# S4D block in front of a feed-forward net: the written order on GpSimd, the initial sums after the odd sines, and a setup in three parts

## The chip, the cores and the metric

The kernel runs on one core of one Trainium2 chip. The metric is the device time of one execution in microseconds; less is better. The three runs shown below took 1494.46, 1496.56 and 1498.57 us; their median, 1496.56 us, is the time before. The profile was taken of a further execution, which took 1500.85 us.

A core has a matrix engine (TensorE, PE in the profile; its weight loads are PEld), VectorE (DVE), ScalarE (ACT), GpSimd (POOL) and SyncE (SP), which only issues transfers here. Each engine works through its own queue in order; an instruction whose input is not there yet holds up all that is queued behind it.

## The reference

```python
mod = (silu(c) @ w_mod)                      # 6 vectors of 576: sa, ca, ga, sb, cb, gb
dt = exp(log_dt);  A = -exp(log_A_real) + 1j*A_imag;  C = (C_real + 1j*C_imag)*dt
P = exp((A*dt)[:, :, None] * pos)            # 576 channels x 128 states x 2048 positions
K = 2*einsum("dn,dnl->dl", C, P).real        # one filter of 2048 taps for each channel
h = layernorm(x)*(1+ca) + sa
x = x + ga*(causal_convolution(h, K) + h*D_skip)
h = layernorm(x)*(1+cb) + sb
x = x + gb*(relu(h @ w1) @ w2)               # 2048 x 576, inner width 4608
```

All is in float32.

## The kernel before

The positions are cut into four blocks of 512. Kernel block 0 (the first 512 taps of all filters, class KGen) is computed first, in about 197 us; then the convolution of block 0, and then the feed-forward net, during which the filters and convolutions of the later blocks run beside the matrix products. This text is about the first 197 us.

**Groups.** The 576 channels are six groups of 96; g is the group. A complex power exp((A dt) l) is taken apart by position: l is written as the sum of a part that W1 holds (positions in steps of 32, 16 of them) and a part that W2 holds (32 offsets around it). The products of the two, summed over the 128 states, are matrix products.

**One group goes through these steps.**
- `turns(g)`: matrix products of angles (`zt`) with a diagonal of positions (`dl`) give the angle in turns in a PSUM bank (tile `ph`); ScalarE rounds it to an integer (`k`), VectorE subtracts (line 143). Six chunks, two in each of three tiles.
- `exps(g)`: ten chunks of matrix products with `zr`; ScalarE takes the exponential (`E`).
- `values(g)`: sines and cosines on ScalarE; the sine products with E on VectorE (lines 179 and 180), the cosine products on GpSimd (lines 184 and 185), once for odd and once for even positions. For the odd ones `start` also makes the first entry of W1, out of the coefficients `cc`: `tc` on GpSimd (line 201), `Tc` on VectorE (line 202), and the two initial sums on VectorE (lines 203 and 204). `powers` makes the multipliers `Zp` and `zs`.
- `doubling(g)`: W1 grows from one entry to 16 in four steps, each two products and two sums. The sums of the last step, in two halves u0 and u1, are done by GpSimd (lines 246 and 247), all others by VectorE.
- `products(g)`: 384 small matrix products (line 255), the first 192 from u0 and the others from u1, into one PSUM bank (`kps`). `rows` copies it out (`ke`).

**The written order** in `first` is: the loads of `mod` and silu(c), spread over a tile `cb`; turns and exps of group 0; the product for ga (`mps_ga`); values(0); turns and exps of group 1; the product for ca (`mps_ca`). Then for each g: doubling(g), products(g) (for g = 0 the product for sa, `mps_sa`, follows), values(g+1), turns and exps of g+2.

**What sets the real order.** A scheduler goes through the program with a model of the machine; of what the model holds to be ready, an engine gets the instruction that is written first. So an engine's queue can differ from the written order. `keep_in_program_order` ties an instruction behind the one that was written before it on its engine. Before the change, only ScalarE's activations in this stage are tied (helper `act`, line 49; all of them have that line in the profile).

**Shared buffers.** Three PSUM banks `ph` serve turns, exps, the mod products and `kps`. The sine tile `s` has one buffer, so the even sines wait until the odd sine products have read it. The tag W1 has two buffers: the weights `wm_ga` and `wm_ca` lie in them before W1 of groups 0 and 1.

Of the kernel before, what the change touches and what calls it, by code (L numbers as in the profile page):

```python
# [18 lines left out]
P = 128  # L19
# [20 lines left out]
class KGen:  # L40
# [7 lines left out]
    def act(self, *args, **kw):  # L48
        return self.tc.keep_in_program_order(self.nc.scalar.activation(*args, **kw))
# [10 lines left out]
    def setup(self, I):  # L60
        nc, pc, k = self.nc, self.pc, self.k
        v = nc.vector.tensor_tensor
        tmp = lambda n: self.pt.tile([G, NG, P], F32, tag="W2", bufs=5, name=n)
# [17 lines left out]
        th = self.pt.tile([G, NG, P], F32, tag="T1", bufs=2, name="th")  # L81
        z = [pc.tile([G, 2, NG, P], F32R, name=f"z{n}") for n in "tr"]
        v(ai, ai, dtb, op=ALU.mult)
        nc.vector.tensor_scalar(th, ai, TURN_LO, None, op0=ALU.mult)
        nc.vector.scalar_tensor_tensor(th, ai, TURN_HI, th, op0=ALU.mult, op1=ALU.add)
        self.act(z[0][:, 0], th, AF.Copy)
        self.diag(lv, slice(0, 8))
        v(z[0][:, 1], th, z[0][:, 0], op=ALU.subtract)
# [7 lines left out]
        self.zz = z  # L96
        self.act(dt, dt, AF.Exp)
        for r in range(2):
            nc.vector.scalar_tensor_tensor(
                self.cc[:, r], self.cc[:, r], 2.0 - 4.0 * r, dt, op0=ALU.mult, op1=ALU.mult  # L100
            )

    def diag(self, lv, sl):
        n = sl.stop - sl.start
        self.nc.vector.tensor_tensor(
            self.dl[:, sl],
            self.k.ident[:G, :G].unsqueeze(1).broadcast_to([G, n, G]),
            lv[:, sl].unsqueeze(2).broadcast_to([G, n, G]),
            op=ALU.mult,
        )  # L110
# [46 lines left out]
    def half_values(self, g, W2, E, f, odd):  # L157


        nc = self.nc  # L160
        v, p = nc.vector.tensor_tensor, nc.gpsimd.tensor_tensor
        j0 = 0 if odd else 16
# [11 lines left out]
        if odd:  # L174
            self.start(g, su[:, :, 7], c[:, 7])
        for u in range(2):
            uc = slice(u * H, u * H + H)
            hi, lo = slice(j0 + 8, j0 + 16), slice(j0, j0 + n)
            v(W2[u][:, 1, hi], su[:, u], Eh[:, :, uc], op=ALU.mult)
            nc.vector.scalar_tensor_tensor(  # L180
                W2[u][:, 1, lo][:, ::-1], su[:, u, 0:n], -1.0,
                El[:, 0:n, uc][:, ::-1], op0=ALU.mult, op1=ALU.mult,
            )
            p(W2[u][:, 0, hi], c[:, :, uc], Eh[:, :, uc], op=ALU.mult)
            p(W2[u][:, 0, lo][:, ::-1], c[:, 0:n, uc], El[:, 0:n, uc][:, ::-1], op=ALU.mult)
            if not odd:
                nc.gpsimd.tensor_copy(W2[u][:, 0, 23], El[:, 7, uc])
                nc.gpsimd.memset(W2[u][:, 1, 23], 0.0)

    def start(self, g, s15, c15):  # L190

        v, p = self.nc.vector.tensor_tensor, self.nc.gpsimd.tensor_tensor
        W1 = self.W1[g] = self.pt.tile([P, 2, 16, 2, H], F32, tag="W1", bufs=2, name=f"W1_{g}")
# [8 lines left out]
        v(T, cc, s15.unsqueeze(1).broadcast_to(cb), op=ALU.mult)  # L202
        v(W1[:, :, 0, 0], t[:, 0], T[:, 1], op=ALU.add)
        v(W1[:, :, 0, 1], t[:, 1], T[:, 0], op=ALU.subtract)

    def powers(self, g, e, f):

        v, p = self.nc.vector.tensor_tensor, self.nc.gpsimd.tensor_tensor
        Z = self.ps.tile([P, 2, 512], F32, tag="Z", name=f"Zp_{g}")[:, :, 0 : 4 * G]
# [12 lines left out]
    def doubling(self, g):  # L222

        v, p = self.nc.vector.tensor_tensor, self.nc.gpsimd.tensor_tensor
        W1, Z = self.W1[g], self.Z[g][0]
# [36 lines left out]

    def first(self, mod):

# [160 lines left out]
class Body:  # L425
# [3 lines left out]
    def build(self):  # L429
        nc, tc, I = self.nc, self.tc, self.I  # L430
        with ExitStack() as ctx:
# [14 lines left out]
            with ExitStack() as c2:  # L446
                kg.open(c2)
                kg.setup(I)
                kg.first(self.mod(kg))
            self.main(ctx, kg)  # L450
# [16 lines left out]
    def mod(self, kg):  # L467
# [17 lines left out]
        self.mod_lhs(cb)  # L485
        yield
        self.m = {}
# [592 lines left out]
```

## Time and profile before

| | us |
|---|---|
| median of three runs | 1496.56 |
| the profiled execution, device time | 1500.85 |
| its span, first to last instruction | 1499.0 |
| kernel block 0, to the last copy of `ke` | 0 to 193.4 |
| products of groups 0 to 5 begin at | 49.9, 82.0, 108.0, 134.4, 161.7, 179.5 |
| TensorE busy / VectorE / ScalarE / GpSimd, whole span | 88% / 62% / 32% / 11% |

In rows of the timeline the first two numbers are the start and the length in us, then come engine, line, operation, output<-inputs, shape and count; in brackets stands how long the engine had been idle and what ended that. A row with a count merges neighbours; its length goes from the start of the first to the end of the last. "issue" is a wait that no semaphore explains. In rows of the windows view each engine has its busy time and its instructions; after them come the granted TensorE clock, the share of time that the transfer engines were busy, and GB/s.

### The profile page before, as it was taken

How to read it: one execution, taken by the hardware profiler on the slowest of the kernel's cores; microseconds unless marked ns; L12 is line 12 of the kernel's file. 1: busy time of each engine (PE TensorE's matmuls, PEld its weight loads, DVE VectorE, ACT ScalarE, POOL GpSimd, SP SyncE). 2: the span in 40 equal slices, each digit the busy share in tenths (PEclk: the TensorE clock that was granted, in tenths of full speed). 3: DMA queues.
4: the chain of work that ended last, by engine and by line, in shares of the span. 5: the costliest groups of instructions: out<-in, count | busy, mean ns of one | idle time of the engine just before them, and what ended most of it. 6: DMA issues, size and time to landing. Idle time of an engine off the chain costs nothing.

```text
span 1499.0 us, 26182 instructions
## 1 busy us (share of the span) xinstructions
PE 1314.2 (88%) x10664; PEld 1037.4 (69%) x10664; DVE 928.2 (62%) x1392; ACT 481.4 (32%) x889; POOL 168.7 (11%) x271
## 2 busy tenths in 40 slices
PE   5976547599998996788999998999999999999997
PEld 3665434477776764566777776787787888888885
DVE  6576649899946398684884597727599822111112
ACT  5475432222221242133223422334322333233331
POOL 2346500000021100001101000000000000000000
PEclk9755569699999998789999999999999999999998
DMA  4535666367598664647976889566799566766662
GB/s 157 212 154 218 229 230 244 136 230 268 182 351 315 212 244 186 258 150 265 354 239 228 314 304 357 165 215 206 283 324 385 173 184 203 210 194 194 198 191 72
DMA packets 118120, 345.99 MB, mean 231 GB/s; under 512 B 19633, under 2 KB 23377, under 8 KB 106993
## 3 DMA queue, kind: packets, MB, share of 16 engines
q1 hardware_dynamic: 99648, 218.88, 44.8%
q0 software_dynamic: 18128, 124.86, 22.1%
q8 instruction: 83, 1.36, 0.4%
q10 hardware_dynamic: 224, 0.59, 0.1%
q14 instruction: 37, 0.30, 0.1%
HBM read 260.53 MB, written 83.76 MB: 230 GB/s over the span
## 4 chain that ended last, share of the span: by engine, by line
PE 43%; DVE 23%; issue 19%; DMA 9%; ACT 3%; POOL 1%; SPq 0%; POOLq 0%; ACTq 0%; DVEq 0%
PE acc L902 15%; PE hps L877 14%; PE kps L381 4%; DVE T L742 4%; DVE Y L744 4%; PE ps_f L613 3%; PE ph L117 3%; DMA Ud<-U 2%; PE kps L255 2%; DMA L1d<-w 1%; PE ps_i L751 1%; DMA kt<-kd 1%; DMA Ua<-Ud 1%; DVE T L350 1%; DVE Y L738 1%
## 5 line engine op out<-in xcount | busy, mean ns | idle before, releaser
L902 PE MATMUL acc<-hh,w 128*128 128x512 f32 x1296 | 428.6, 405 | 4.7 <-DMA w<-L2d 3.7
L877 PE MATMUL hps<-xh,w 128*128 128x512 f32 x1152 | 394.5, 403 | 0.0
L902 PE MATMUL acc<-hl,w 128*128 128x512 f32 x720 | 283.5, 407 | 20.3 <-DVE hl L883 20.3
L883 DVE SCALAR_TENSOR_TENSOR hl<-hps,hh 128x512 fp32r<-128x512 f32 x144 | 98.8, 686 | 310.5 <-ACT hh L882 310.2
L902 PEld LDWEIGHTS acc<-hh,w 128*128 128x128 f32 x1296 | 245.9, 191 | 59.7 <-DMA w<-L2d 4.5
L877 PEld LDWEIGHTS hps<-xh,w 128*128 128x128 f32 x1152 | 219.0, 191 | 47.5
L877 PE MATMUL hps<-xl,w 128*128 128x512 f32 x576 | 232.3, 403 | 0.0
L882 ACT ACTIVATE hh<-hps 128x512 fp32r<-128x512 f32 x144 | 86.1, 598 | 353.2 <-PE hps L877 349.8
L860 ACT ACTIVATE w<-r 128x576 fp32r<-128x576 f32 x144 | 98.8, 686 | 278.0 <-issue 183.9
L902 PEld LDWEIGHTS acc<-hl,w 128*128 128x128 f32 x720 | 137.2, 191 | 50.7 <-DVE hl L883 21.5
L877 PEld LDWEIGHTS hps<-xl,w 128*128 128x128 f32 x576 | 110.3, 192 | 23.8
L851 ACT ACTIVATE w<-r 128x640 fp32r<-128x640 f32 x144 | 105.4, 732 | 24.4 <-DMA L1d<-w 20.5
L877 PE MATMUL hps<-xs,w 128*128 128x512 f32 x288 | 101.0, 420 | 10.8 <-DMA w<-L1d 5.2
L381 PEld LDWEIGHTS kps<-W1r,W2r 128*32 128x32 f32 x3456 | 68.8, 146 | 39.3 <-issue 28.3
L381 PE MATMUL kps<-W1r,W2r 128*32 128x48 f32 (+2 forms) x3456 | 79.5, 238 | 14.3 <-issue 12.3
L744 DVE TENSOR_TENSOR Y<-Y,T 128x1152 f32<-128x1152 f32 x64 | 84.5, 1347 | 0.1
L255 PE MATMUL kps<-W,W 128*32 128x16 f32 x2304 | 42.0, 218 | 42.6 <-issue 21.2
L614 ACT ACTIVATE Z<-ps_f 128x288 f32<-128x288 f32 x128 | 51.7, 409 | 70.7 <-PE ps_f L613 67.9
L255 PEld LDWEIGHTS kps<-W,W 128*32 128x32 f32 x2304 | 39.2, 151 | 47.3 <-issue 22.2
L877 PEld LDWEIGHTS hps<-xs,w 128*128 128x128 f32 x288 | 54.0, 192 | 25.7 <-DMA w<-L1d 6.8
L1000 POOL DMA_DIRECT2D out_dram<-x x16 | 8.7, 546 | 511.9 <-DVE x L998 511.9
L613 PE MATMUL ps_f<-kt,fcK 128*128 128x288 f32 x128 | 45.0, 450 | 21.2 <-DMA wm_sb<-in_w_mod_dram 15.5
(177 smaller groups left out, 1545.4 us busy)
## 6 DMA issues: line engine op xcount, KB each, us to landing
r<-in_w_dram SPq DMA_DIRECT2D x144, 320.0 KB, 3.7
r<-in_w_dram SPq DMA_DIRECT2D x144, 288.0 KB, 3.5
w<-L1d SPq DMA_DIRECT2D x108, 320.0 KB, 3.1
w<-L2d SPq DMA_DIRECT2D x108, 288.0 KB, 3.2
W2r<-W2d POOLq DMA_DIRECT2D x18, 1536.0 KB, 9.0
W2d<-W SPq DMA_DIRECT2D x12, 1536.0 KB, 7.2
Ua<-Ud POOLq DMA_DIRECT2D x15, 1152.0 KB, 10.5
W<-W1d POOLq DMA_DIRECT2D x18, 768.0 KB, 10.2
```

The costliest lines, as they stand in the source:

```text
L255: self.nc.tensor.matmul(ps[32 * dd : 32 * dd + 32, 12 * u + q, :], W2[:, r, :, ch], W1[:, u, :, r, ch], start=(r == 0), stop=(r == 1),)
L381: nc.tensor.matmul(ps[32 * dd : 32 * dd + 32, q, :], W2[:, r, :, ch], W1[:, :, r, ch], start=(r == 0), stop=(r == 1),)
L613: nc.tensor.matmul(o, fc[:, n2, c, :], src(n2), start=True, stop=True)
L614: nc.scalar.activation(Z[:, n2, c], ps[:, :PC], AF.Copy)
L742: v(T, k, u, op=ALU.mult)
L744: v(y, y, T, op=op or ALU.add)
L851: nc.scalar.activation(w[:, 0], r, AF.Copy)
L860: nc.scalar.activation(w[:, 0:D], r, AF.Copy)
L877: nc.tensor.matmul(ps, a, x, start=(i == 0), stop=(i == 13))
L882: nc.scalar.activation(hh, ps, AF.Relu)
L883: nc.vector.scalar_tensor_tensor(hl, ps, 0.0, hh, op0=ALU.max, op1=ALU.subtract)
L902: nc.tensor.matmul(acc[i], a, x, start=(f == 0 and j in (0, 3, 6, 9, 12)), stop=(f == NF - 1 and j in (2, 5, 8, 11, 13)),)
```

## The change

- GpSimd's two-input operations in this stage (`start`, `half_values`, `powers`, `doubling`) are tied to the written order. So the u1 sums of doubling(g) come ahead of `tc` and of the cosine products of group g+1, and these ahead of the sums of doubling(g+1).
- In the odd half of `values`, the initial sums (lines 203 and 204) are written behind the four odd sine products, and the cosine products after them. The sums themselves stay free.
- The setup is cut in three. What turns(0) needs stays in front and is tied in order. Part 2 (the decay rates `lar`, `zr`, two pieces of the diagonal) comes between turns(0) and exps(0). Part 3 (exp of dt, the coefficients `cc`) comes after exps(0).
- In `mod`, the exponential of c, the rest of silu and `cb` move behind the first `yield`: after part 3, ahead of the product for ga.

```diff
+    def pool(self, out, a, b, op):
+        self.tc.keep_in_program_order(self.nc.gpsimd.tensor_tensor(out, a, b, op=op))
...
-        v(ai, ai, dtb, op=ALU.mult)
-        nc.vector.tensor_scalar(th, ai, TURN_LO, None, op0=ALU.mult)
-        nc.vector.scalar_tensor_tensor(th, ai, TURN_HI, th, op0=ALU.mult, op1=ALU.add)
+        kept(v(ai, ai, dtb, op=ALU.mult))
+        kept(nc.vector.tensor_scalar(th, ai, TURN_LO, None, op0=ALU.mult))
+        kept(nc.vector.scalar_tensor_tensor(th, ai, TURN_HI, th, op0=ALU.mult, op1=ALU.add))
         self.act(z[0][:, 0], th, AF.Copy)
         self.diag(lv, slice(0, 8))
-        v(z[0][:, 1], th, z[0][:, 0], op=ALU.subtract)
+        kept(v(z[0][:, 1], th, z[0][:, 0], op=ALU.subtract))
         self.diag(lv, slice(16, 25))
-        nc.vector.scalar_tensor_tensor(lar, lar, -1.0, dtb, op0=ALU.mult, op1=ALU.mult)
-        self.act(z[1][:, 0], lar, AF.Copy)
         self.diag(lv, slice(32, NS))
-        v(z[1][:, 1], lar, z[1][:, 0], op=ALU.subtract)
-        self.diag(lv, slice(8, 16))
-        self.diag(lv, slice(25, 32))
...
+        def part2():
+            kept(nc.vector.scalar_tensor_tensor(lar, lar, -1.0, dtb, op0=ALU.mult, op1=ALU.mult))
+            self.act(z[1][:, 0], lar, AF.Copy)
+            v(z[1][:, 1], lar, z[1][:, 0], op=ALU.subtract)
+            self.diag(lv, slice(8, 16))
+            self.diag(lv, slice(25, 32))
+
+        def part3():
+            self.act(dt, dt, AF.Exp)
+            for r in range(2):
+                nc.vector.scalar_tensor_tensor(
+                    self.cc[:, r], self.cc[:, r], 2.0 - 4.0 * r, dt, op0=ALU.mult, op1=ALU.mult
+                )
+
+        return part2, part3
...
-        v, p = nc.vector.tensor_tensor, nc.gpsimd.tensor_tensor
+        v, p = nc.vector.tensor_tensor, self.pool
...
         if odd:
-            self.start(g, su[:, :, 7], c[:, 7])
+            ends = self.start(g, su[:, :, 7], c[:, 7])
         for u in range(2):
             ...
             v(W2[u][:, 1, hi], su[:, u], Eh[:, :, uc], op=ALU.mult)
             nc.vector.scalar_tensor_tensor(...)
+        if odd:
+            for out, a, b, op in ends:
+                v(out, a, b, op=op)
+        for u in range(2):
+            uc = slice(u * H, u * H + H)
             p(W2[u][:, 0, hi], c[:, :, uc], Eh[:, :, uc], op=ALU.mult)
...
         def raw(g, then=lambda: None):
             F = self.turns(g, then)
+            if g == 0:
+                setup[0]()
             EF[g] = self.exps(g), F
+            if g == 0:
+                setup[1]()
...
             self.mod_weights(w, slice(i * D, (i + 1) * D))
+        yield
         kg.act(ex, ct, AF.Exp, scale=-1.0)
...
         self.mod_lhs(cb)
-        yield
```

`diag` ties its product in the same way, and `start` hands its two sums back instead of issuing them.

More of the change, by code (lines that the diff above doesn't have):

```diff
@@ L81, in setup @@
         th = self.pt.tile([G, NG, P], F32, tag="T1", bufs=2, name="th")
-        z = [pc.tile([G, 2, NG, P], F32R, name=f"z{n}") for n in "tr"]
-        v(ai, ai, dtb, op=ALU.mult)
-        nc.vector.tensor_scalar(th, ai, TURN_LO, None, op0=ALU.mult)
-        nc.vector.scalar_tensor_tensor(th, ai, TURN_HI, th, op0=ALU.mult, op1=ALU.add)
+        z = self.zz = [pc.tile([G, 2, NG, P], F32R, name=f"z{n}") for n in "tr"]
+        kept(v(ai, ai, dtb, op=ALU.mult))
+        kept(nc.vector.tensor_scalar(th, ai, TURN_LO, None, op0=ALU.mult))
@@ L94, in setup @@
-        self.diag(lv, slice(8, 16))
-        self.diag(lv, slice(25, 32))
[L96 to L101, printed above, removed]
+        def part2():
[4 more added lines that the diff above has]
+            self.diag(lv, slice(25, 32))
@@ L103, in diag @@
+        def part3():
[5 more added lines that the diff above has]
+        return part2, part3
     def diag(self, lv, sl):
         n = sl.stop - sl.start
[L105 to L109, printed above, removed]
+        self.tc.keep_in_program_order(
+            self.nc.vector.tensor_tensor(
+                self.dl[:, sl],
+                self.k.ident[:G, :G].unsqueeze(1).broadcast_to([G, n, G]),
+                lv[:, sl].unsqueeze(2).broadcast_to([G, n, G]),
+                op=ALU.mult,
+            )
@@ L202, in start @@
         v(T, cc, s15.unsqueeze(1).broadcast_to(cb), op=ALU.mult)
-        v(W1[:, :, 0, 0], t[:, 0], T[:, 1], op=ALU.add)
-        v(W1[:, :, 0, 1], t[:, 1], T[:, 0], op=ALU.subtract)
+        return (
+            (W1[:, :, 0, 0], t[:, 0], T[:, 1], ALU.add),
+            (W1[:, :, 0, 1], t[:, 1], T[:, 0], ALU.subtract),
+        )
     def powers(self, g, e, f):
-        v, p = self.nc.vector.tensor_tensor, self.nc.gpsimd.tensor_tensor
+        v, p = self.nc.vector.tensor_tensor, self.pool
         Z = self.ps.tile([P, 2, 512], F32, tag="Z", name=f"Zp_{g}")[:, :, 0 : 4 * G]
@@ L222, in doubling @@
     def doubling(self, g):
-        v, p = self.nc.vector.tensor_tensor, self.nc.gpsimd.tensor_tensor
+        v, p = self.nc.vector.tensor_tensor, self.pool
         W1, Z = self.W1[g], self.Z[g][0]
@@ L261, in products, with first @@
                     )
-    def first(self, mod):
+    def first(self, setup, mod):
         nc, k = self.nc, self.k
@@ L447, in build @@
                 kg.open(c2)
-                kg.setup(I)
-                kg.first(self.mod(kg))
+                setup = kg.setup(I)
+                kg.first(setup, self.mod(kg))
             self.main(ctx, kg)
```

6 lines of the change are left out of this document (3 added, 3 removed).

## Prediction

> **What bounds the kernel now.** I read the page first, then the windows view by stages, then the chain of waits and the timeline of the first 200 us. After 260 us nothing of the change runs, and TensorE is busy for 1147 of 1239 us; what the first stage gains or loses is carried to the end one for one. So only the first 193 us count.
>
> ```profile
> span 1499.0 us, 26182 instructions
> ...
> 260.00:1499.00 1239.00, 1147.12 (x7968) 906.09 (x7968) 755.23 (x1034) 355.30 (x656) 76.97 (x137) 0.96 0.70 236
> ```
>
> The first stage is a relay. TensorE's products(g) are followed by turns(g+2) in TensorE's own queue; VectorE's queue has the subtractions of these turns ahead of most of doubling(g+1); this leads to GpSimd's sums and to products(g+1). The next rows show the products of groups 1, 2 and 3.
>
> ```profile
> 88.45 2.36 PE L255 MATMUL kps<-W,W 128*32 128x16 f32 x128 [2.31 <-issue]
> ...
> 93.10 1.40 PE L255 MATMUL kps<-W,W 128*32 128x16 f32 x68 [2.29 <-issue]
> ...
> 113.54 0.94 PE L255 MATMUL kps<-W,W 128*32 128x16 f32 x39 [2.05 <-issue]
> 115.15 1.60 PE L255 MATMUL kps<-W,W 128*32 128x16 f32 x89 [0.67 <-POOL W L247]
> 117.85 1.87 PE L255 MATMUL kps<-W,W 128*32 128x16 f32 x101 [1.10 <-issue]
> ...
> 135.37 3.10 PE L255 MATMUL kps<-W,W 128*32 128x16 f32 x190
> 139.84 0.30 PE L255 MATMUL kps<-W,W 128*32 128x16 f32 x2 [1.38 <-POOL W L246]
> 140.80 2.95 PE L255 MATMUL kps<-W,W 128*32 128x16 f32 x183 [0.66 <-POOL W L247]
> 146.61 0.42 PE L255 MATMUL kps<-W,W 128*32 128x16 f32 x7 [2.86 <-issue]
> ```
>
> TensorE stalls after each run of 128 products (x128, and 39 + 89) without a semaphore, and runs begin 4.65 (88.45 to 93.10) or 4.31 us (113.54 to 117.85) apart. 128 products with their loads are 256 instructions; the queue of instruction loading moved 20 packets in this stage:
>
> ```profile
> q8 instruction: 20, 0.33, 0.7%
> ```
>
> So I read these stalls as the loading of the next 256 instructions, and a run of products as bound by it at some 4.3 to 4.7 us per 128. A sum that comes earlier inside a run buys nothing.
>
> **GpSimd's order.** No work is added. In group 3 the u0 sums end at 135.32 and the u1 sums' inputs are there by then, but `tc` and two cosine products come first:
>
> ```profile
> 134.32 1.00 POOL L247 TENSOR_TENSOR W<-T,T 128x384 f32<-128x384 f32 x1
> 136.25 0.62 POOL L201 TENSOR_TENSOR tc<-cc,c 128x192 f32<-128x192 f32 x1 [0.93 <-ACT c L49]
> ```
>
> Tied, the u1 sums follow at 135.3 and end at 137.2, while now they release TensorE at 140.80; `tc` starts at 137.2, 1.0 later; what is queued behind the cosine products ends 1.0 earlier, since the idle 0.93 is used. Who waits for `tc` is VectorE's line 203, which moves back too. SP's queue gets the store of W1 some 3.5 us earlier and the one of W2 no later; nothing in this stage reads them. For TensorE: group 1 had no wait for GpSimd, gain 0. In group 2 the wait (0.67) lies within the run that began at 113.54, and the next comes 4.31 later anyway: 0. In group 3 the waits are 1.38 + 0.66. The run that ends in the 2.86 stall began 128 products before 143.75, at about 141.7; without the waits it could begin when its instructions are there, one spacing (4.3) after the run before it (119 products in, 137.3), at 141.6. That makes a gain of 0.1 at least and 2.0 at most; I take 1.0, since 141.7 showed no stall and the loading may have been done well before. Group 4's products are followed by no turns, so its gain lies on no path. **−1.0** (−2.0 to 0).
>
> **Initial sums behind the odd sines.** For the last groups VectorE waits for `tc` in the middle of the odd sine products, and ScalarE's even sines wait for the last of these:
>
> ```profile
> 162.45 0.55 DVE L179 TENSOR_TENSOR W<-s,E 128x384 f32<-128x384 f32 x1
> 164.20 0.26 DVE L203 TENSOR_TENSOR W<-tc,Tc 128x96 f32<-128x96 f32 x1 [1.21 <-POOL tc L201]
> ...
> 164.54 0.55 DVE L180 SCALAR_TENSOR_TENSOR W<-s,E 128x384 f32<-128x384 f32 x1
> ...
> 166.05 0.81 ACT L49 ACTIVATE s<-k 128x768 f32<-128x768 f32 x1 [1.90 <-DVE W L180]
> ```
>
> Behind the sines, line 180 follows line 179 at 162.92 (0.47 from start to start) instead of 164.54: 1.6 earlier. In groups 1 to 3 what ends earlier (multipliers, ScalarE's queue) then waits for TensorE's turns: nothing gained. After group 4 there are no more turns: even sines, multipliers, doubling(5) and products(5) hang on it in line: **−1.6** (0 if the sums stay early, at most the 1.90).
>
> **Setup.** These rows carry it:
>
> ```profile
> 5.14 0.56 DVE L84 TENSOR_SCALAR th<-ai 96x768 f32<-96x768 f32 x1
> 6.19 0.84 ACT L49 ACTIVATE lar<-lar 96x768 f32<-96x768 f32 x1 [2.63 <-DMA lar<-in_lar_dram]
> 7.94 0.95 DVE L85 SCALAR_TENSOR_TENSOR th<-ai,th 96x768 f32<-96x768 f32 x1
> 9.81 0.95 DVE L88 TENSOR_TENSOR zt<-th,zt 96x768 fp32r<-96x768 f32 x1
> 10.41 0.67 ACT L49 ACTIVATE dt<-dt 128x576 f32<-128x576 f32 x1
> 10.68 1.72 DVE L105 TENSOR_TENSOR dl<-ident,lv 96x864 fp32r<-96x864 f32 x2
> 11.54 0.87 ACT L49 ACTIVATE k<-ph 128x384 int32<-128x384 f32 x2 [0.37 <-PE ph L117]
> 14.83 1.42 DVE L99 SCALAR_TENSOR_TENSOR cc<-cc,dt 128x576 f32<-128x576 f32 x2
> 16.24 0.55 DVE L143 TENSOR_TENSOR k<-ph,k 128x384 f32<-128x384 f32 x1
> 17.77 0.81 DVE L513 COPY cb<-ct 128x640 f32<-128x640 f32 x1
> 18.50 1.27 DVE L143 TENSOR_TENSOR k<-ph,k 128x384 f32<-128x384 f32 x3
> 19.10 5.95 PE L117 MATMUL ph<-dl,zr 96*128 96x384 f32 x20 [0.29 <-DVE k L143]
> 20.14 5.40 ACT L49 ACTIVATE E<-ph 128x384 f32<-128x384 f32 x10 [0.89 <-PE ph L117]
> 24.99 5.70 PE L518 MATMUL mps_ga<-wm_ga,cb 128*128 128x288 f32 x20
> 26.85 0.81 ACT L49 ACTIVATE s<-k 128x768 f32<-128x768 f32 x1
> ```
>
> Line 85 follows line 84 at 5.7 and ends at 6.6. ScalarE's copy to zt waits for `lar` (7.03) and, like it, takes 0.84: 7.9. Line 88 ends at 8.85, the two pieces of the diagonal (1.72) at 10.5. The first k came 0.78 after line 88's end, so at 9.6. The first subtraction thus starts at 10.5, not 16.24; all six took 3.5 (to 19.77), so they end at 14.0. Then part 2, alone on the path: multiply 0.95, copy 0.84, subtract 0.95, with TensorE idle: exps(0) at 16.8, not 19.10, **2.3 earlier**. E ends at 23.2. Behind it ScalarE now has dt (0.67) and the small exponential of c (five columns, an estimated 0.1), which ran under VectorE's setup before; the sines, 1.31 after E now, start at 25.3, **1.5 earlier** than 26.85.
>
> The cover that is gone is that of `cb`. dt is done at 23.8, `cc` takes 1.42, three small steps an estimated 0.4, `cb` 0.81: 26.4, so `mps_ga` starts 1.4 later than now, and TensorE idles from 22.7 to 26.4. What an idle stretch like that does to its clock shows here:
>
> ```profile
> 35.62 1.97 PE L117 MATMUL ph<-dl,zt 96*128 96x384 f32 x6 [3.67 <-DVE k L143]
> ...
> 59.47 10.04 PE L518 MATMUL mps_sa<-wm_sa,cb 128*128 128x288 f32 x20
> ```
>
> ```profile
> 34.30:44.20 9.90, 8.37 (x26) 7.71 (x27) 9.57 (x24) 7.60 (x16) 4.68 (x7) 0.50 0.77 318
> ...
> 59.50:68.50 9.00, 9.00 (x20) 5.52 (x18) 2.38 (x6) 0.00 (x0) 0.89 (x2) 0.50 0.81 308
> ```
>
> After 3.67 idle the granted clock was 0.50 until 44.2, and `mps_sa`, the same 20 products as `mps_ga`, took 10.04 at 0.50 against 5.70. I take 10.04, the nearest row: `mps_ga` ends at 36.4 instead of 30.69. Turns(1) are next in TensorE's queue and can't go around it. Now they wait for ScalarE:
>
> ```profile
> 34.19 1.22 ACT L49 ACTIVATE k<-ph 128x384 int32<-128x384 f32 x3
> ```
>
> Then they would wait for TensorE: first k at 37.2 (0.78 after the start), the fourth chunk 1.43 after it (34.19 to 35.62): 38.6, +3.0. The chunks then run at the full clock, −0.3 (an estimate: a third off the 1.97 of six, half of it on the path). Ahead of the first subtraction VectorE may have the second copy of ga and the initial sums, which wait for `mps_ga` too (W1 lies in the buffer of `wm_ga`), and even sines and multipliers behind them: 0 to 1.5, I take 0.4. Exps(1), `mps_ca` and products(0) follow as they are: **+3.1** (−1.5, with no cold start, to +4.2).
>
> **Sum.** +3.1 − 1.0 − 1.6 = +0.5: the span from 1499.0 to 1499.5, the profiled execution from 1500.85 to 1501.35. The median of the runs shown, 1496.56, lies 4.29 below that execution: **1497.1**.
>
> **Rivals.**
> 1. The head start survives. If TensorE is warm for `mps_ga` (5.70: end 32.1), turns(1) start with ScalarE's queue, 1.5 early: −1.5 − 2.6 = −4.1, **1492.5**. For it: ScalarE's queue is 1.5 early in any case. Against: the clock fell after each idle stretch of over 2 us above.
> 2. The clock comes back within `mps_ga`. The `zr` products began at 19.10, and `mps_ga` behind them, from 24.99, ran at full speed; so the clock came back within 5.9 us. Then 11.8 products run at 0.50 each and 8.2 at 0.285 (5.70 / 20): the end is 34.6, the setup +1.3, the time **1495.3**. Against: `mps_sa` stayed at 0.50 for all of 9 us. The Trainium skill ("TensorE: Matmul & The Clock Gate", Part 1: The HAM clock gate) speaks against the change first: the array falls to half rate after an idle window of some 3.4 us. It adds that one busy window of that length releases it. By that, an estimate, `mps_ga` would end at 33.6 and the time be 1494.3; the row of `mps_sa` bears out the first half of the rule and not the second.
> 3. Instruction loading doesn't bind. Then the u1 waits fall away in full: 2.0 in place of 1.0 in group 3 and 0.67 in group 2: 1.7 less, **1495.4**. Against: in the run at 88.45 no engine was waited for. The Trainium skill ("Runtime: NRT & Kernel Launch", Instruction fetch mechanics) would have it so: it calls the cost of crossing a block of 256 instructions mostly hidden. The stalls of 2.05 to 2.86 after 128 products disagree.
> 4. Slower: VectorE's queue. Now the first copy of ga stands ahead of the odd sine products and held them:
>
> ```profile
> 27.91 0.46 DVE L495 COPY m_ga<-mps_ga 128x288 f32<-128x288 f32 x1 [8.14 <-PE mps_ga L518]
> ...
> 30.53 0.81 ACT L49 ACTIVATE s<-k 128x768 f32<-128x768 f32 x1 [0.39 <-DVE W L180]
> ```
>
>  If both copies stand ahead of the odd sines, these start only at 36.9, their even successors on ScalarE at 39.1 instead of 30.53, and all behind it is 8.6 late: 8.6 − 2.6 = +6.0, **1502.6**. With one copy ahead it is +1.7. It decides from the point at which the even sines start after 37. Against: the model that sets the order sees `cb` late as well.
> 5. It doesn't do what it says: the sums of lines 203 and 204 are not tied and may stay early; then the 1.6 is not gained: **1498.7**.
>
> **How the numbers follow.** Chances: forecast 0.38, rival 1 0.14, rival 2 0.15, rival 3 0.06, rival 4 0.16, rival 5 0.11. The likeliest gives 1497.1; with its own bounds (setup +1 to +4.2, gains 0.5 to 3.5) it reaches from 1494 to 1500.3. The range goes to rival 4 and a little below rival 1: 1491.5 to 1502.6. Faster or slower counts from 0.3% (4.5 us), about what a measurement of this kernel tells from no change: below 1492.1 lie half of rival 1 and the edge of the others, 0.13; above 1501.0 most of rival 4 and a tail of the forecast, 0.19; the rest is 0.68.
>
> **What would show it.** First subtraction (line 143) near 10.5, `zr` products near 16.8, first sines near 25.3; `mps_ga` starting near 26.4 at a clock of 0.50 and ending near 36; products(0) near 53. From group 1 on no cosine product between the sums, products 4.3 to 4.7 per 128 as before, and line 203 behind the sines, with the last two stretches 1.6 shorter. The prediction is wrong if TensorE is warm at `mps_ga`, if VectorE's queue holds sines behind the copies of ga, if products of groups 1 or 2 shrink, or if the stage after 260 us changes.

## The result, and the profile after

| kernel | runs | median us | ratio to before, 95% interval |
|---|---|---|---|
| before | 20 | 1497.57 | |
| changed | 20 | 1499.04 | 1.0008 (0.9987 to 1.0029) |

No difference that can be measured: +1.2 us by the ratio, between −1.9 and +4.3. The forecast was 1497.1 and "the same". The profiled execution of the changed kernel has a span of 1497.1 us and a time of 1499.16. That the sum came out is luck: two of its three terms were far off, with opposite signs, as the single parts show below.

The next rows are the timeline of the changed kernel up to products(0): start, busy time, engine, line, operation, count, and in brackets the idle time before it and what ended that.

```profile
10.69 1.59 DVE L153 TENSOR_TENSOR k<-ph,k 128x384 f32<-128x384 f32 x3
...
26.01 0.82 DVE L534 COPY cb<-ct 128x640 f32<-128x640 f32 x1
...
25.41 0.81 ACT L49 ACTIVATE s<-k 128x768 f32<-128x768 f32 x1
...
37.77 1.25 ACT L49 ACTIVATE k<-ph 128x384 int32<-128x384 f32 x3 [5.03 <-PE ph L127]
```

```profile
26.93 10.26 PE L539 MATMUL mps_ga<-wm_ga,cb 128*128 128x288 f32 x20 [3.94 <-ACT s L49]
...
52.49 0.29 PE L272 MATMUL kps<-W,W 128*32 128x16 f32 x2 [0.25 <-POOL W L52]
```

The windows view puts the granted clock (the number after POOL) beside the stretch in which `mps_ga` ran:

```profile
26.30:36.40 10.10, 9.47 (x18) 5.54 (x18) 6.00 (x13) 6.12 (x10) 8.36 (x10) 0.50 0.14 58
36.60:43.20 6.60, 5.18 (x23) 3.36 (x24) 5.31 (x15) 4.86 (x10) 0.73 (x3) 1.00 0.97 386
```

The first subtraction is at 10.69 in place of 16.24, and the sines at 25.41 in place of 26.85. `cb` is there at 26.83 (the bracket of `mps_ga` names ScalarE's `s`, but that was done at 26.22); `mps_ga` runs from 26.93 to 37.19, at 0.50 until 36.5, and ScalarE waits 5.03 for turns(1) where it waited for nothing before. Products(0) start at 52.49 in place of 49.92.

Group 3 in the changed kernel, beside which the prediction shows before's rows from 135.37 on:

```profile
135.32 3.87 PE L272 MATMUL kps<-W,W 128*32 128x16 f32 x247
140.72 2.17 PE L272 MATMUL kps<-W,W 128*32 128x16 f32 x128 [1.53 <-issue]
144.18 0.43 PE L272 MATMUL kps<-W,W 128*32 128x16 f32 x7 [1.29 <-issue]
```

Neither wait for GpSimd is left, the stall of 2.86 ahead of the last seven products has become 1.29, and products(3) take 10.25 (134.36 to 144.61) in place of 12.62. In the tail ScalarE's even sines wait 0.46 for VectorE in place of 1.90:

```profile
162.02 0.82 ACT L49 ACTIVATE s<-k 128x768 f32<-128x768 f32 x1 [0.46 <-DVE W L190]
```

The windows by stage, before first and then the changed kernel. The first row of each ends where the last `ke` does, the second begins with the load of x.

```profile
0.00:193.85 193.85, 128.01 (x2556) 105.26 (x2556) 119.60 (x261) 106.58 (x186) 85.57 (x125) 0.68 0.52 194
197.71:1499.00 1301.29, 1186.19 (x8108) 932.18 (x8108) 808.17 (x1131) 374.85 (x703) 83.12 (x146) 0.95 0.70 237
```

```profile
0.00:190.44 190.44, 127.85 (x2556) 102.59 (x2556) 120.23 (x261) 106.27 (x186) 85.54 (x125) 0.69 0.53 197
194.30:1497.10 1302.80, 1190.49 (x8108) 932.76 (x8108) 808.95 (x1131) 374.87 (x703) 82.84 (x146) 0.95 0.69 236
```

In this one execution block 0 is 3.41 us shorter and the stage behind it, in which every queue has the same order as before, is 1.51 longer. Over all profiled executions of this study the time from the end of block 0 to the end of the span lay between 1301.0 and 1312.4, with no clear relation to the length of block 0. So one execution can't weigh 3 us, and block 0 has to be read by its distances, over many kernels.

### The profile page after: what moved, and what is told of

It is laid out like the page before. It is cut to its first block, busy times and chain, and to the rows that moved or that the text cites. A ratio compares the mean times of both kernels' runs of the same rounds, so it can differ in the third digit from the quotient of the medians.

```text
span 1497.1 us, 26176 instructions
## 1 busy us (share of the span) xinstructions
PE 1318.3 (88%) x10664; PEld 1035.3 (69%) x10664; DVE 929.6 (62%) x1392; ACT 481.1 (32%) x889; POOL 168.4 (11%) x271
## 4 chain that ended last, share of the span: by engine, by line
PE 41%; DVE 19%; issue 19%; DMA 9%; ACT 1%; POOL 1%; SPq 0%; POOLq 0%; DVEq 0%; ACTq 0%
PE acc L923 15%; PE hps L898 15%; PE kps L402 4%; DVE T L763 4%; DVE Y L765 3%; PE ps_f L634 3%; DMA Ud<-U 2%; DMA Ua<-Ud 2%; DMA w<-L2d 2%; PE ps_i L772 1%; DMA kt<-kd 1%; DVE hl L904 1%; DVE Y L759 1%; DMA L1d<-w 1%; DVE T L371 1%
## 6 DMA issues: line engine op xcount, KB each, us to landing
W<-W1d POOLq DMA_DIRECT2D x18, 768.0 KB, 10.5
```

## The experiments

Two tables hold the distances. "Products(g)" is the start of group g's first product; times in us. The "stores' edit" is the kernel before with W1's stores written later; all its queues up to the end of block 0 hold the same instructions in the same order as before's, so it serves as a second execution of before.

| kernel | GpSimd tied | sums behind sines | products(1) to (4) | products(4) to (5) | products(5) to end of `ke` |
|---|---|---|---|---|---|
| before | no | no | 79.77 | 17.76 | 14.37 |
| setup alone, 2 executions | no | no | 78.87, 80.39 | 17.72, 17.52 | 14.34, 14.34 |
| stores' edit | no | no | 79.38 | 17.63 | 14.61 |
| sums alone | no | yes | 82.04 | 16.13 | 15.74 |
| tie alone, 2 executions | yes | no | 75.87, 76.57 | 18.28, 18.30 | 13.23, 13.01 |
| changed kernel | yes | yes | 76.54 | 16.20 | 14.99 |
| its 5 variants in the setup or the stores | yes | yes | 75.91 to 77.88 | 16.18 to 16.20 | 14.90 to 15.23 |
| its variant with the u1 sums twice | yes | yes | 77.70 | 16.20 | 14.95 |

| kernel | `mps_ga` starts | takes | products(0) |
|---|---|---|---|
| before | 24.99 | 5.70 | 49.92 |
| changed | 26.93 | 10.26 | 52.49 |
| setup alone, 2 executions | 26.67, 26.59 | 7.32, 7.80 | 51.43, 50.81 |
| changed, u1 sums twice (same setup) | 26.20 | 10.11 | 53.28 |
| changed, W1's stores twice (same setup) | 26.77 | 7.85 | 48.90 |
| changed, silu in front | 26.91 | 6.55 | 54.25 |
| changed, 14 matmuls ahead of `mps_ga` | 26.56 | 5.67 | 47.07 |
| changed, silu between | 22.47 | 6.64 | 49.94 |
| silu between, 14 matmuls behind `mps_ga` | 22.46 | 5.67 | 48.55 |

The distance from products(0) to products(1) is left out of the first table, since it goes with the clock at `mps_sa`, which lies in it: it was 32.03 in before, where `mps_sa` took 10.04, and 27.52 in the stores' edit, where the same 20 products took 5.70.

```profile
59.09 5.70 PE L518 MATMUL mps_sa<-wm_sa,cb 128*128 128x288 f32 x20
```

In the sums alone it was 27.10, again with 5.70. So the profile shown of before is one of its longer ones: its block 0 ends at 193.85, that of the stores' edit at 188.85. A comparison with the 193.85 alone can be wrong by 5 us, more than any term of the prediction.

### The tie alone

Before, with GpSimd's operations issued through the tied helper and nothing else.

```diff
-        v, p = nc.vector.tensor_tensor, nc.gpsimd.tensor_tensor
+        v, p = nc.vector.tensor_tensor, self.pool
```

> The kernel before with the first part of the change alone: GpSimd tied to the written order. The setup and the initial sums are as before. The prediction's step: from products(1) to products(4) 1.0 less than the 79.77 of before (78.8; bounds 77.8 to 79.8), all of it between products(3) and products(4); from products(4) to the end of ke 32.1 as before. Rival (in the changed kernel's 76.54 the initial sums' move has the larger part): 79 to 79.8 here, and the shortening shows with the sums alone. Rival (the tie does it all): 76.5 to 77.5 here.

> The kernel before with GpSimd's tie alone, as in an earlier look in which block 0 ended at 187.33 in place of 193.85 and products(1) to the end of ke took 107.38 in place of 111.90. Theory (the tie is the part that gains, whatever state the clock is in): 4 to 5 us less than before, a ratio of 0.9965 to 0.9975. Rival (the look was a lucky one): a ratio within 0.999 to 1.001.

Measured: 75.87 and 76.57 from products(1) to products(4), and a median of 1494.55 against 1498.20, ratio 0.9971 (0.9952 to 0.9990): −4.3 us. This is the part that gains, four times what the prediction gave it. By groups, over the five untied and the eight tied executions without doubled sums, the mean distance fell from 26.11 to 25.88 (group 1), 26.94 to 25.54 (group 2) and 27.04 to 25.23 (group 3). The prediction had 0, 0 and −1.0. Single distances of group 1 spread over 2.2 untied and 1.5 tied, so that nothing can be said of its part.

### The u1 sums twice

The changed kernel, with these lines added behind the last doubling, so that the u1 sums end 2 us later.

```diff
+                if m == 8 and u.start == 1 and g in (1, 2, 3):
+                    add(out[:, u, :, 0], t[:, :, :, 0], T[:, :, :, 1], op=ALU.subtract)
+                    add(out[:, u, :, 1], t[:, :, :, 1], T[:, :, :, 0], op=ALU.add)
```

> The changed kernel with GpSimd's sums of the second half (u1, the last doubling) of groups 1, 2 and 3 written twice, with the same result: what TensorE waits for is some 2 us later in each of the three groups. It only adds work. Theory (runs of 128 products are set by the loading of instructions): the starts of products(2), (3) and (4) move by less than 0.7 us each against products(1), 1.5 in all at most, since the second half of each group's products begins behind a loading stall anyway. Rival (the u1 sums gate TensorE): each of the three moves by 1.5 to 2 us, block 0 ends 4 to 6 us later.

Measured: 25.78, 26.75 and 25.18 in place of 26.38, 25.26 and 24.90: +1.2 in all for 6 us of added sums, though group 2 alone moved by 1.5, beyond the 0.7 expected of each. TensorE's rows in group 3, products from 138.31:

```profile
139.26 3.25 PE L275 MATMUL kps<-W,W 128*32 128x16 f32 x192
143.17 1.04 PE L275 MATMUL kps<-W,W 128*32 128x16 f32 x53 [0.66 <-POOL W L52]
144.41 2.16 PE L275 MATMUL kps<-W,W 128*32 128x16 f32 x128 [0.20 <-issue]
148.42 0.43 PE L275 MATMUL kps<-W,W 128*32 128x16 f32 x9 [1.85 <-issue]
```

The wait of 0.66 takes the place of the loading stall (0.20 left of 1.53), and products(3) take 10.54, 0.29 more than 10.25. This is the prediction's reading: a wait inside a run that the loading holds costs next to nothing. What it missed is how much loading itself would shorten.

### Why the loading may be faster with the tie

The stalls are not of a fixed length. Below is the DMA digit row (busy share of the 16 engines in tenths, slices of 0.25 us) from 4 us behind the start of products(3), first of before (from 138.41), then of the changed kernel (from 138.36).

```profile
DMA  0000000000006999999910020000090959999793
```

```profile
DMA  9999995110000200000000000909094989899691
```

The run of 9s is the store of W1's second half. Tied, it is over at 140.0; untied, it fills the engines from 141.4 to 143.4. The lone 2 is the packet of 256 instructions (the only one of the instruction queue in these 10 us): at 144.2 before, after the store; at 141.8 in the changed kernel. 2.4 later in both the last products start (146.61 and 144.18). In before the last whole run began at about 141.7, in the changed kernel at 140.72, so the packet came 2.5 into the run in the one and 1.1 in the other. The reading: the tie, by ending the u1 sums 3.5 us earlier, moves the store off the loading.

The two executions of the setup alone, with GpSimd untied, point the same way. In both the run of 128 products of group 1 has the store beside it. These are the digits from the start of that run, at 86.71 in the first and 87.08 in the second:

```profile
DMA  0000989999970000000300009792919191939899
```

```profile
DMA  0049999999200200000000095999969492909091
```

In the first the store begins 1.0 into the run; the packet came at 1.2, just behind its beginning, and the last products 3.83 after the run's start. In the second the store begins 0.4 earlier, and the packet (the later 2, at 90.4) came only behind it, 3.3 into the run, the last products after 5.75. In before and in the stores' edit the store begins 1.0 into this run, and the packet came at 2.2 and 1.3: there one order gave spacings of 4.65 and 4.10. In group 2 of the run with the u1 sums twice the store, as late as the sums, fills the engines until 2.0 into the run, and the packet came at 2.3 in place of 1.5. Group 2 of before is another case:

```profile
DMA  0000003007899999910003000095989969593929
```

From 113.54 on, the packet (the first 3, at 115.25) came ahead of the store and right behind the end, at 115.15, of the 0.67 for which TensorE waited for GpSimd. There it is the wait that held up the packet, and the spacing of 4.31 owes nothing to the store.

Two runs were meant to test the reading about the store by moving transfers. The first adds the same stores once more, to the changed kernel:

```diff
-            for u in range(2):
+            for u in (0, 1, 0, 1) if g in (1, 2, 3) else (0, 1):
                 nc.sync.dma_start(
                     out=k.W1d[2 * g + u], in_=self.W1[g][:, u].rearrange("p a r c -> p (a r c)")
                 )
```

> The changed kernel with the stores of W1 of groups 1, 2 and 3 written twice on SP's queue (the same data to the same place; nothing waits for them in this stage). It only adds transfers. Theory (instruction loading shares the DMA engines with the stores: where these had 0.02 to 0.3 of the 16 engines, the last run of 128 products followed the one before it after 3.46 to 3.84 us; where they had 0.42 to 0.45, as in the kernel before, after 4.31 to 4.65): the DMA share behind the first run rises to 0.4 to 0.9 and the spacing of the last runs of groups 1, 2 and 3 to between 4.3 and 5.9; from products(1) to products(4) 2 to 7 us more than 76.54. Rival (the tie works by what TensorE waits for on GpSimd, transfers don't matter): spacings and the 76.54 stay within 1 us.

The expectation missed: the spacings stayed at 3.83, 3.83 and 3.73, and products(1) to (4) at 76.81. The same view, from 4 us behind its products(3) (133.19):

```profile
DMA  9999997999999931310099899999995939290919
```

The added stores end at 136.7 and the next ones begin at 138.2; the packet (the 3 at 137.3) came in the gap. So the mean DMA share, which was 0.68 to 0.73 over the three spacings here, says nothing, and the run neither supports the theory nor speaks against it. The second put the stores, in the kernel before, behind those of the next group:

```diff
-            for u in range(2):
-                nc.sync.dma_start(
-                    out=k.W1d[2 * g + u], in_=self.W1[g][:, u].rearrange("p a r c -> p (a r c)")
-                )
...
             if g + 1 < NG:
                 values(g + 1)
+            for u in range(2):
+                nc.sync.dma_start(
+                    out=k.W1d[2 * g + u], in_=self.W1[g][:, u].rearrange("p a r c -> p (a r c)")
+                )
```

> The kernel before with one edit: the stores of W1 of a group are issued on SP's queue behind the stores of the next group's W2 and Z in place of ahead of them. GpSimd's order stays untied, so TensorE's waits for its sums stay too. Theory (the tie's gain is mostly that W1's stores no longer fall on the loading of the last run): the spacing of the last runs of groups 1 and 2 falls from 4.65 and 4.31 to 3.4 to 3.9, products(1) to products(3) from 52.46 to 50.7 to 51.5; group 3 keeps its waits of 1.38 and 0.66 and may gain less; products(1) to (4) 77.5 to 79. Rival (the tie works by the sums' earlier end alone): 79 to 80.5, spacings as before.

Measured 79.38, spacings 4.1 and 4.64. But the order in which SP executed them did not change: the stores of W1 still went out ahead of W2's, 0.9 and 6.7 us after the start of products(1), as in before. It is one more execution of the old order, not a test. That a saturating transfer delays the loading is thus read from where packets fall beside stores, and not shown by an experiment.

### The sums alone

Before, with the two initial sums issued behind the odd sine products.

```diff
-            self.start(g, su[:, :, 7], c[:, 7])
+            ends = self.start(g, su[:, :, 7], c[:, 7])
...
+            for out, a, b, op in ends:
+                v(out, a, b, op=op)
```

> The kernel before with the second part of the change alone: the two initial sums issued behind the odd sine products. GpSimd's order and the setup are as before. The prediction's step: nothing from products(1) to products(4) (79.77), and 1.6 less from products(4) to products(5): 16.2 in place of 17.76, with the even sines' wait on ScalarE falling from 1.90 to about 0.5. Rival (the tie is what brings it: without it tc is late as before and the sums wait behind the sines, where they hold the even ones no less): 17.5 to 17.8. Rival (the move works in groups 2 and 3 too): products(1) to (4) falls to 77.5 to 78.5.

Products(4) to (5) fell by 1.63, as predicted to the tenth. But the stretch behind it grew by 1.37, and on top of the tie it is the same: −2.1 (18.29 to 16.20, means of the two) and then +1.9 (13.12 to 14.99). The gain is given back inside products(5). Here are the last two runs of products(5) with the tie alone, and then in the changed kernel:

```profile
182.17 2.13 PE L258 MATMUL kps<-W,W 128*32 128x16 f32 x128 [3.73 <-issue]
185.90 0.90 PE L258 MATMUL kps<-W,W 128*32 128x16 f32 x42 [1.59 <-issue]
```

```profile
183.33 2.17 PE L272 MATMUL kps<-W,W 128*32 128x16 f32 x128 [3.54 <-issue]
188.97 0.94 PE L272 MATMUL kps<-W,W 128*32 128x16 f32 x42 [3.48 <-issue]
```

And the DMA digits from 4 us behind the start of products(5) in each (from 178.1, and from 179.5):

```profile
DMA  9989999999989999999352212000000000020000
```

```profile
DMA  9999999999899999999999999998511111000000
```

The stores of W1 and W2 and the three loads that GpSimd's queue issues here fill the engines until 182.9 in the one and 186.5 in the other. The last 42 products start 3.0 and 2.5 after that. Measured from the start of products(4), 155.81 and 159.26, the transfers end at 27.1 and 27.2: not moved, while products(5) start at 18.29 and 16.20. So products that start earlier meet the same transfers, and wait for their instructions. From products(1) to (4) the sums alone came to 82.04, 2.3 more than before; a single execution, whose products(2) took 13.80 in place of 11.70, and with the tie nothing of the kind shows (76.54 against 75.87 and 76.57).

### The setup alone

Before, with the setup split and the silu of c behind exps(0); GpSimd and the sums as before.

```diff
-                kg.setup(I)
-                kg.first(self.mod(kg))
+                setup = kg.setup(I)
+                kg.first(setup, self.mod(kg))
```

> The kernel before with the third part of the change alone: setup split around the first phases, the silu of c behind exps(0); GpSimd's order and the initial sums are as before. Prediction by its parts: first subtraction near 10.6, sines near 25.4, mps_ga 27 to 37, products(0) near 53, 2.6 to 3.1 later than before; what follows group 1 keeps its distances, so that block 0 ends 2.5 to 3 us later than before, near 196.5. Rival (the delay is taken up by slack in groups 1 to 3, as the distance of 0.77 at products(1) suggests): block 0 ends within 1 us of 193.85.

> The kernel before with the setup split alone, as in an earlier look in which products(0) started 1.51 later than before and products(1) 1.70 earlier. Prediction's step: 3.1 us slower in the median, a ratio of 1.001 to 1.003; that and 4 to 5 us from the tie would leave the whole change near no difference. Rival (what is lost by products(0) is taken up by products(1), as in the look): a ratio of 0.998 to 1.0005.

Measured: median 1503.70 against 1498.20, ratio 1.0039 (1.0018 to 1.0060): +5.8 us. It is the part that loses, and more than +3.1. In the two profiled executions products(0) are 1.5 and 0.9 later than before, not 2.6 to 3.1, and block 0 ends at 191.19 and 192.61, between the 188.85 and the 193.85 of before's order. Where the 5.8 of the median lie is not settled: in the second of them the time behind block 0 was 1312.4, the longest of all, with all queues in before's order there. `mps_ga`, from the second:

```profile
26.59 7.80 PE L532 MATMUL mps_ga<-wm_ga,cb 128*128 128x288 f32 x20 [3.94 <-ACT s L49]
```

The edit also changes TensorE's queue: two of the `mps_sa` products come in between products(0), as in the changed kernel. `mps_ga` took 7.32, 7.80 and 7.85 in three of the five executions with this setup, and 10.11 and 10.26 in two: the products went at full pace from 3 to 5 us after its start in the three, and from some 9 to 10 in the two. (In the first setup execution 7 products fill the 3.20 us from 26.70, and 14 the 3.80 from 30.10. The windows view prints 1.00 for both: the records of the clock begin at 30.0 there, so this is read from the pace.) Products(0) lay between 48.90 and 53.28 in these five, at 51.4 in the mean, and between 49.71 and 51.24, at 50.3, in the five executions with the setup of before.

### Which half of the setup's loss is the clock

The changed kernel, with work that nobody reads in TensorE's idle stretch:

```diff
+                warm = self.bank("warm")[:, : 4 * G].rearrange("p (s c) -> p s c", c=G)
+                for i in range(14):
+                    nc.tensor.matmul(warm, self.zz[0][:, 0, 0], self.dl[:, 0:4], start=True, stop=True)
                 setup[1]()
```

> The changed kernel with 14 matmuls more, of operands that are there and into a bank that nobody reads, between exps(0) and mps_ga on TensorE: some 4.2 us of work (14 of 0.30) in the 4 us in which TensorE idles. It only adds work. Theory (the cold clock is most of the loss): the granted clock stays at 1.0, mps_ga still starts near 27, takes 5.7 in place of 10.26 and ends near 32.7; turns(1) follow, products(0) near 48 in place of 52.49. Rival (the late start alone is the loss, or the clock falls for another reason than the idle stretch): the clock falls all the same, mps_ga takes 8 to 10 and products(0) stays within 1.5 us of 52.49.

```profile
22.42 3.33 PE L293 MATMUL warm<-dl,zt 96*128 96x384 f32 x14
26.56 5.67 PE L542 MATMUL mps_ga<-wm_ga,cb 128*128 128x288 f32 x20 [0.82 <-ACT s L49]
...
34.04 0.62 PE L127 MATMUL ph<-dl,zt 96*128 96x384 f32 x2 [0.55 <-DVE k L153]
```

```profile
26.60:32.20 5.60, 5.60 (x21) 3.43 (x21) 4.20 (x10) 5.28 (x10) 4.52 (x6) 1.00 0.00 0
32.20:47.00 14.80, 13.03 (x53) 8.31 (x52) 13.33 (x32) 12.53 (x23) 5.89 (x9) 1.00 0.59 228
```

`mps_ga` starts as late as in the changed kernel and takes 5.67 in place of 10.26, the clock stays at 1.00 until products(0), and these start at 47.07, 5.4 earlier. The median is 1492.44 against 1498.08, ratio 0.9950 (0.9925 to 0.9975). So the cold clock is the loss at products(0), and the head start of the setup is real once the clock is kept. By the medians the matmuls bring more, some 8.7 us against the changed kernel (−7.5 and +1.2 to before); where the rest comes from is open. The Trainium skill ("TensorE: Matmul & The Clock Gate", Part 1: The HAM clock gate) says that an idle window of some 3.4 us halves the clock, that one busy window brings it back, and that windows run free of the kernel. The first and the last agree with 10.26 against 5.67 here, and with 7.32 to 10.26 for one and the same setup; the second does not hold for the 10.1 us at 0.50 in the changed kernel.

### Where the silu could stand

In front again, as in before, in the changed kernel:

```diff
-        yield
         kg.act(ex, ct, AF.Exp, scale=-1.0)
...
         self.mod_lhs(cb)
+        yield
```

> The changed kernel with one step put back where it stood before the change: the silu of c and its copy cb are made in VectorE's setup again, and no longer behind exps(0). Nothing else differs, and the result is complete. Theory (late cb, then a cold clock): cb is there before exps(0) ends, so mps_ga follows exps(0) at once, at about 23, at the full clock, takes 5.7 in place of 10.26 and ends near 28.7 in place of 37.19. Turns(1) then wait for ScalarE's queue alone, which is free at about 33.5: the fourth chunk's k near 34.5 in place of 38.9, products(0) near 48 in place of 52.49, some 4.5 us earlier. The price of the step in front is 0.8 to 1.0 on the first subtraction (11.5 in place of 10.69). Block 0 ends near 187 in place of 190.44. Rival (the late start of mps_ga is not what sets products(0), the queue of VectorE behind it is): products(0) stays within 1 us of 52.49. Rival (what block 0 gains is lost in the stage after it): block 0 is 3 to 4 us shorter and the span is not.

This missed: products(0) at 54.25, and a ratio of 0.9984 (0.9966 to 1.0002).

```profile
9.81 0.21 ACT L49 ACTIVATE ex<-ct 128x5 f32<-128x5 f32 x1 [1.87 <-DMA ct<-in_c_dram]
```

```profile
10.05 0.17 DVE L502 TENSOR_SCALAR ex<-ex 128x5 f32<-128x5 f32 x1 [3.66 <-ACT ex L49]
...
14.80 1.47 DVE L153 TENSOR_TENSOR k<-ph,k 128x384 f32<-128x384 f32 x3
```

VectorE's tied queue holds the diagonal behind these steps, and stands idle 3.66 for the transfer of c; the first subtraction comes at 14.80 in place of 10.69 and the `zr` products at 20.09, behind the 19.10 of before: the whole head start is gone. Behind the second part of the setup VectorE has room instead:

```diff
             if g == 0:
                 setup[0]()
+                next(mod)
...
         self.mod_lhs(cb)
+        yield
```

> The changed kernel with the silu of c and its copy cb put between the second part of the setup and exps(0), where VectorE idles for 5.48 before cc in the changed kernel. It leaves nothing out. Theory (what the move cost is the late cb with the idle stretch behind it, and c's DMA, landing near 9.8, is what must not be waited for in front): the first subtraction stays near 10.7, exps(0) near 16, the sines at 25.2; cb is there near 19.5, so mps_ga follows exps(0) without a gap at 22.7 and ends at 28.4 (33 if the clock is low); turns(1) wait for ScalarE alone, fourth chunk near 34.3, products(0) at 47 to 48.5 in place of 52.49, block 0 ends at 185 to 186.5. The ratio to before near 0.995. Rival (VectorE's queue now has both copies of ga within the odd sines and is held by them): products(0) after 50. Rival (the stage behind gives it back): block 0 is shorter and the time is not.

```profile
18.75 0.82 DVE L536 COPY cb<-ct 128x640 f32<-128x640 f32 x1
```

```profile
22.47 6.64 PE L541 MATMUL mps_ga<-wm_ga,cb 128*128 128x288 f32 x20
29.04 1.33 PE L127 MATMUL ph<-dl,zt 96*128 96x384 f32 x6
35.19 1.97 PE L127 MATMUL ph<-dl,zt 96*128 96x384 f32 x6 [4.82 <-DVE k L153]
```

`mps_ga` follows exps(0) without a gap, as expected, and the ratio is 0.9957 (0.9940 to 0.9975). Products(0), though, start at 49.94 and not at 47 to 48.5: now TensorE idles 4.82 behind the first turns(1), its clock falls there (0.50 in the second row of the windows below), the 20 `zr` products run at it, and `mps_ca`, which is ahead of products(0) in TensorE's queue, starts at 43.79, against 41.11 in the run with the 14 matmuls.

```profile
29.00:34.70 5.70, 1.37 (x7) 1.01 (x6) 4.25 (x11) 4.60 (x10) 5.70 (x7) 1.00 0.01 1
34.90:45.00 10.10, 9.60 (x29) 8.66 (x30) 9.80 (x24) 7.77 (x16) 2.13 (x4) 0.50 0.82 315
```

The last kernel adds the 14 matmuls at that place:

```diff
+        for i in range(14):
+            nc.tensor.matmul(warm, self.zz[0][:, 0, 0], self.dl[:, 0:4], start=True, stop=True)
         values(0)
```

> The kernel of the run before this one with 14 matmuls more into a bank that nobody reads, behind mps_ga on TensorE (some 4 us, while it waits for turns(1)). It only adds work. Theory (the granted clock falls after an idle stretch of a whole 3.4 us and costs turns(1), exps(1) and mps_ca some of their time): the clock stays at 1.0 until products(0), which start 0.5 to 2 us earlier than without them. Rival (these steps are set by ScalarE and VectorE): products(0) stays within 0.5 us.

Products(0) start at 48.55, 1.4 earlier; the clock stays at 1.0 only until 36.3, not until products(0). The ratio, 0.9962 (0.9943 to 0.9981), is no better than without. The three kernels with ratios of 0.9950, 0.9957 and 0.9962 beat both the kernel before and the changed one. They cannot be told from each other, nor from the tie alone (0.9971, up to 0.9990).

## Why the prediction was right, and where it was not

The total held because two terms were too small with opposite signs: measured one by one in medians, the tie is −4.3 (prediction −1.0), the setup +5.8 (+3.1), and what is left for the sums, 1.2 + 4.3 − 5.8, is −0.3 (−1.6), the last with an uncertainty of some 5 us.

- **What bounds it.** That runs of products are held by the loading of instructions was right: 2 us of later u1 sums cost next to nothing. The Trainium skill ("Runtime: NRT & Kernel Launch", Instruction fetch mechanics) calls this cost mostly hidden; the stalls of 1.29 to 3.73 in the rows above disagree. The step that failed is the fixed spacing, "some 4.3 to 4.7 us per 128". In groups 1 to 4 it is 3.45 to 4.10 where data transfers hold less than a tenth of the DMA engines' time; beside stores it reaches 5.75. In products(5) it is 3.73 with the tie alone and 5.09 to 5.92 in the other kernels.
- **GpSimd's order**, −1.0, was mis-sized: −3.4 from products(1) to (4) in the means. Group 1's 0 is not contradicted (−0.2). Group 2's 0 failed (−1.4): "the next comes 4.31 later anyway" took for fixed what the wait had lengthened, as the packet at 115.25 shows. Group 3's −1.0 was −1.8, within its bounds. The prediction saw that SP's queue "gets the store of W1 some 3.5 us earlier" and wrote that nothing reads it; it asked who reads the data, and not what else the transfer delays.
- **Sums behind the odd sines**, −1.6: the place and the size were right at the start of products(5) (−1.6 alone, −2.1 on the tie), and "carried to the end" was wrong: products(5) give it back. Of the cover, "what is late next" was left out there.
- **Setup.** First subtraction 10.5 forecast, 10.69 measured; sines 25.3 and 25.41; `mps_ga` 26.4 for 10.04 to 36.4, and 26.93 for 10.26 to 37.19; fourth chunk 38.6 and 38.91; products(0) +3.1 and +2.57. Only the `zr` products, 16.8, came at 15.99. In its own execution every other step held, and part of that is luck: the row taken for the price, `mps_sa` at 10.04, took 5.70 in two other executions of the same order, and `mps_ga` 7.32 to 7.85 in three of five with this setup. What was missed is that the cold stretch is not the same length in each execution.
- **One for one.** The time behind block 0 varies by more than any of these terms in single executions, so "gains or loses is carried to the end one for one" can only be held against medians. The tie's distance from products(1) to the end of `ke` (107.38 and 107.88, against 111.90 in before and 111.62 in the stores' edit) is 3.7 to 4.5 shorter, which agrees with its −4.3; the setup's two executions and its +5.8 do not, and that stays open.
- **Rivals.** 1 (no cold clock) did not happen in the changed kernel, but the run with 14 matmuls shows its price, 5.4 at products(0). 2 (the clock comes back within `mps_ga`) is what three of the five executions with this setup show. 3 was wrong about loading, and with −2.7 for the tie nearer to what was measured. 4: the first copy of ga held one of VectorE's even sine products by 1.13, behind ScalarE's even sines and not ahead of them; nothing came of it. 5 did not happen.

## What to carry to other kernels

A step moved off the path can cost more by the idle stretch that it leaves on TensorE than by its own time: ask which engine's work it was hiding, and whether the clock survives. A store or a load that nobody waits for may not be free where many small instructions are being loaded; look where it lies against the stalls. A second profile of the same order can differ by 5 us in a stage of 190: don't build on one. And a change that measures as nothing may be a gain and a loss: time its parts alone before giving it up, since here the tie by itself is worth 0.3%. With the silu in its free place the setup no longer costs this; that it adds to it is not shown.

## What the runs showed of the hardware

With the DMA engines nearly idle around it, the packet of 256 instructions comes 1.1 to 1.6 us into the run of products before (140.72 to 141.8 in the changed kernel), and the first of its products start 2.2 to 3.2 after it; beside stores it came up to 3.6 into the run, and with the engines full to 186.5 the stall ahead of 42 products was 3.48. And the cold clock lasted 3 to 5 us into `mps_ga` in three executions of one setup and 9 to 10 in two others, so a term that hangs on it has no single value.
